# Seven-product (Strassen) GEMMs in three of four MLP layers, in four passes over the tokens

## The chip, the cores and the metric

The kernel runs on one core of one Trainium2 chip. The metric is the device time of one execution in microseconds (us). A run of the program is timed on its own; a profile of one execution shows the span from its first to its last instruction, and everything below that names a row is of that profile. The engines are TensorE (PE, whose weight loads the profile lists as PEld), VectorE (DVE), ScalarE (ACT), GpSimd (POOL) and SyncE (SP); here SP issues every DMA.

## The reference

The input is q, k and v, each 8 batches x 8 heads x 576 tokens x 64, in float32, and four weight matrices that arrive as float64 words. With 8 heads of 64 side by side a token has 512 features, and there are 4608 tokens.

```python
q_s = softmax(q, over the 64)          # per token and head
k_s = softmax(k, over the 576 tokens)  # per head and feature
x   = q_s @ (k_s.T @ v)                # per batch and head, then 4608 x 512
g   = h * sigmoid(1.702 * h),  h = x @ moe_w_in      # 512 -> 2048
x1  = g @ moe_w_out                                  # 2048 -> 512
g   = where(h >= 1, h, where(h <= -1, 0, (h + 1)**2 / 4)),  h = x1 @ moe2_w_in
out = g @ moe2_w_out
```

So four GEMMs of 4608 x 512 x 2048 carry the arithmetic. They are called in1, out1, in2 and out2 here.

## The kernel before, in words

The kernel is written in a tile framework. Python code lists the operations; the framework then fixes, ahead of time, an order of instructions for each engine (which need not be the order of the code), and puts in the semaphore waits. On the chip each engine works through its own list in that order.

Every GEMM operand is split into a high and a low part (`split`, L70 to L72: ACT rounds the high part into the type fp32r, DVE subtracts it from the source). A product is three matmuls: high x high, high x low, low x high. Each has a 128x128 weight and a moving operand of 512 columns.

The tokens are in nine blocks of 512. A step of the main loop belongs to a block and to one of 16 chunks of the hidden layer. `gemm1(s)` (L358 to L360) makes 12 matmuls into one PSUM tile `hps`, `act(s)` and `act_lo(s)` turn it into the split activation `gh`, `gl`, and `gemm2`, two steps behind, makes 12 matmuls (L400) that add the chunk's share to four accumulators. So the hidden activations never leave the core, and the 288 steps (nine blocks of the first MLP, then nine of the second) make 288 x 24 = 6912 matmuls. Only the block's output between the MLPs, `x1`, goes through DRAM.

Beside the steps runs a list of jobs (`at`, sorted by step): the attention of the next block (`chain`: loads, `k_max`, `k_col`, `k_sub`, `k_exp`, `k_v`, `q1` to `q4`), over the 16 steps before the block begins, and the weights. A weight chunk comes as 64-bit words (`load_w`), is made into float32 by one ACT and three DVE instructions (`conv_w`), and is split. The first MLP's weights are converted during the first two blocks, the second's during blocks 2 to 7, and those are kept in DRAM as float32 until the first MLP's last block.

Of the kernel before, what the change touches and what calls it, by code (L numbers as in the profile page):

```python
# [8 lines left out]
FP32 = mybir.dt.float32  # L9
# [9 lines left out]
def kernel(  # L19
# [25 lines left out]
    ACT_Q = (3,)  # L45
    ACT_KV = (0, 1)
    LOWEST = -3.4028234663852886e38
    FAST_K = (0, 1)
    RAW_W = 14
# [4 lines left out]
    wpool = ctx.enter_context(tc.tile_pool(name="w", bufs=2 * NM))  # L54
    xpool = ctx.enter_context(tc.tile_pool(name="x", bufs=2))
    kpool = ctx.enter_context(tc.tile_pool(name="k", bufs=3))
    qpool = ctx.enter_context(tc.tile_pool(name="q", bufs=4))
    qtpool = ctx.enter_context(tc.tile_pool(name="qt", bufs=1))
    sm1 = ctx.enter_context(tc.tile_pool(name="sm1", bufs=1))
    sm = ctx.enter_context(tc.tile_pool(name="sm", bufs=2))  # L60
    sgp = ctx.enter_context(tc.tile_pool(name="sg", bufs=2))
    gp = ctx.enter_context(tc.tile_pool(name="g", bufs=3))
    rawp = ctx.enter_context(tc.tile_pool(name="raw", bufs=1))
    stg = ctx.enter_context(tc.tile_pool(name="stg", bufs=4))
    dram = ctx.enter_context(tc.tile_pool(name="dram", bufs=1, space=bass.MemoryType.DRAM))
    ps_acc = ctx.enter_context(tc.tile_pool(name="ps_acc", bufs=1, space=bass.MemoryType.PSUM))
    ps_h = ctx.enter_context(tc.tile_pool(name="ps_h", bufs=2, space=bass.MemoryType.PSUM))
    ps_a = ctx.enter_context(tc.tile_pool(name="ps_a", bufs=2, space=bass.MemoryType.PSUM))

    def split(hi, lo, src):  # L70
# [3 lines left out]
    ident = const.tile([P, P], FP32, name="ident")  # L74
    NV = 2
    v_t = [const.tile([P, KR + 1, P + 1], FP32, name=f"v{i}") for i in range(NV)]
    kv_t = [const.tile([P, HP, P], FP32, name=f"kv{i}") for i in range(2)]

# [1 line left out]
    w_src = [(w1_in, w1_out), (w2_in, w2_out)]  # L80
    w_raw = {}
    st = {}
    w_f = {}
    w_sb = {}
    w2_dram = [
        [dram.tile([P, DM], FP32, name=f"w2_{io}_{m}") for m in range(NM)] for io in range(2)
    ]

    def load_w(ph, io, m):
        # as long as few weights are there, the others' room takes what comes in  # L90
        if ph == 0 and m < RAW_W:
            t = wpool.tile([P, DM], I64, tag="w", name="wraw")
        else:
            t = rawp.tile([P, DM], I64, tag="raw", name="wraw")
        if io == 0:
            nc.sync.dma_start(
                out=t.rearrange("p (k f) -> p k f", k=KD),
                in_=w_src[ph][0][:, m * P:(m + 1) * P].rearrange("(k p) f -> p k f", p=P),
            )
        else:  # L100
            nc.sync.dma_start(out=t, in_=w_src[ph][1][m * P:(m + 1) * P, :])
        w_raw[ph, io, m] = t

    def conv_w(ph, io, m):
        raw = w_raw.pop((ph, io, m))
# [3 lines left out]
        f = stg.tile([P, DM], FP32, tag="stg", name="wf")  # L109
        r = stg.tile([P, DM], U32, tag="stg", name="wr")  # L110
# [12 lines left out]
        w_f[ph, io, m] = f  # L123

    def store_w2(io, m):
        nc.sync.dma_start(out=w2_dram[io][m], in_=w_f.pop((1, io, m)))

    def load_w2(io, m):
        f = stg.tile([P, DM], FP32, tag="stg", name="wf")
        nc.sync.dma_start(out=f, in_=w2_dram[io][m])  # L130
        w_f[1, io, m] = f

    def split_w(ph, io, m):
        src = w_f[ph, io, m]
        t = wpool.tile([P, 2, DM], FP32R, tag="w", name="w")
        hi, lo = t[:, 0, :], t[:, 1, :]
        nc.scalar.activation(out=hi, in_=src, func=ACTF.Copy)  # L137
        w_sb[ph, io, m] = (hi, lo)

    def split_w_lo(ph, io, m):  # L140
        src = w_f.pop((ph, io, m))
        hi, lo = w_sb[ph, io, m]
        nc.vector.tensor_tensor(out=lo, in0=src, in1=hi.bitcast(FP32), op=ALU.subtract)  # L143

# [1 line left out]
    k_t, q_t = {}, {}  # L146

    # Of a batch's tokens, partition p has KR in a row; one more of the rest is in the first KT.
    def load_tokens(dst, src, together):
        if together:  # L150
            nc.sync.dma_start(out=dst[:, :, :KR], in_=src[:, :KR * P].rearrange("h (p r) d -> p h r d", r=KR))
        else:
            for i in range(2):
                nc.sync.dma_start(out=dst[:, i, :KR], in_=src[i, :KR * P].rearrange("(p r) d -> p r d", r=KR))
        nc.sync.dma_start(out=dst[:KT, :, KR], in_=src[:, KR * P:].rearrange("h p d -> p h d"))

    def load_k(b, hp):
        if b in FAST_K:
            t = wpool.tile([P, 2, KR + 1, D], FP32, tag="w", name="kr").rearrange("p h r d -> p r h d")
        else:  # L160
            t = kpool.tile([P, KR + 1, 2, D], FP32, tag="k", name="kt")
        nc.gpsimd.memset(t[KT:, KR], LOWEST)
        load_tokens(t.rearrange("p r h d -> p h r d"), k[b, 2 * hp:2 * hp + 2], b in FAST_K)
        k_t[b, hp] = t

    def load_v(b, hp):
        if b == 0 and hp >= NV:
            vt = wpool.tile([P, KR + 1, P + 1], FP32, tag="w", name="vf")
            nc.gpsimd.memset(vt[:, :, P:P + 1], 1.0)
        else:  # L170
            vt = v_t[hp % NV]
        load_tokens(
            vt[:, :, :P].rearrange("p r (h d) -> p h r d", h=2), v[b, 2 * hp:2 * hp + 2], False
        )
        st["v", b, hp] = vt

    def segs(t0, size):
        # a stretch of tokens, cut where a batch ends
        done = 0
        while done < size:  # L180
            b, s = divmod(t0 + done, S)
            n = min(size - done, S - s)
            yield done, n, b, s
            done += n

    def load_q(t):
        qt = qpool.tile([P, H, D], FP32, tag="q", name="qt")
        for off, n, b, s in segs(t * P, P):
            nc.sync.dma_start(
                out=qt[off:off + n], in_=q[b, :, s:s + n, :].rearrange("h p d -> p h d")  # L190
            )
        q_t[t] = qt

    def follow(ins, other):
        # keeps the exponentials together: ScalarE changes its table less often
        if other is not None:
            tc.add_manual_dep(
                getattr(ins, "ins", ins),
                getattr(other, "ins", other).name,
                mybir.DependencyInfo(mybir.DependencyClass.NoSync, mybir.DependencyReason.DATA),  # L200
                reason="exponentials together",
            )

    def k_max(b, hp):
        mx = sm1.tile([P, P], FP32, tag="mx", name="mx")
        nc.vector.tensor_reduce(  # L206
            out=mx.rearrange("p (h d) -> p h d", h=2),
            in_=k_t[b, hp].rearrange("p r h d -> p h d r"),
            axis=AX.X,
            op=ALU.max,  # L210
        )
        st["mx", hp] = mx

    def k_col(b, hp):
        pa = ps_a.tile([P, P], FP32, tag="a", name="pa")
        nc.tensor.transpose(out=pa, in_=st.pop(("mx", hp)), identity=ident)  # L216
        mc = sm.tile([P, 1], FP32, tag="mc", name="mc")
        nc.vector.tensor_reduce(out=mc, in_=pa, axis=AX.X, op=ALU.max)
        st["mc", hp] = mc
# [216 lines left out]
    for j in range(2, NB):  # L436
        run(0, j, 0, NM)
# [158 lines left out]
```

## Time and profile before

| what | value |
|---|---|
| three timed runs | 1718.35, 1720.17 and 1722.23 us, median 1720.17 |
| span of the profiled execution | 1716.3 us; the profile gives no time outside the span |
| runs' median less that span | 3.9 us |
| PE busy, matmuls | 98% of the span, 7576 matmul instructions |
| PE weight loads | 81% of the span |
| DVE, ACT busy | 52% and 40% |
| DMA | 109.08 MB on SP's queue, 22.2% of the 16 DMA engines' time |
| chain that ended last | PE 94%, DVE 3%, DMA 2%, ACT 1% |

A busy PE is not a PE at its peak: the end of a matmul is modelled, and the records of one after the other overlap. The pace of matmuls is read from the distance between two starts. The same holds for DVE, where the record of an instruction can reach into the next one's.

### The profile page before, as it was taken

How to read it: one execution, taken by the hardware profiler on the slowest of the kernel's cores; microseconds unless marked ns; L12 is line 12 of the kernel's file. 1: busy time of each engine (PE TensorE's matmuls, PEld its weight loads, DVE VectorE, ACT ScalarE, POOL GpSimd, SP SyncE). 2: the span in 40 equal slices, each digit the busy share in tenths (PEclk: the TensorE clock that was granted, in tenths of full speed). 3: DMA queues.
4: the chain of work that ended last, by engine and by line, in shares of the span. 5: the costliest groups of instructions: out<-in, count | busy, mean ns of one | idle time of the engine just before them, and what ended most of it. 6: DMA issues, size and time to landing. Idle time of an engine off the chain costs nothing.

```text
span 1716.3 us, 19507 instructions
## 1 busy us (share of the span) xinstructions
PE 1686.9 (98%) x7576; PEld 1383.0 (81%) x7576; DVE 895.9 (52%) x1511; ACT 679.2 (40%) x1033; POOL 8.0 (0%) x45
## 2 busy tenths in 40 slices
PE   5899999999999999999999999999999999999999
PEld 4688888888878888888788888888888888888887
DVE  7999438566565756542445343434343434343333
ACT  5885426445354554532444232323232323232222
POOL 0000000000000000000000000000000000000000
PEclk9999999999999999999999999999999999999999
DMA  8661315243241514210233010101010101000000
GB/s 221 174 197 56 85 55 147 59 137 79 68 128 45 151 40 125 56 62 19 92 99 99 1 49 1 50 1 50 0 50 0 50 0 48 2 13 13 3 23 25
DMA packets 155548, 110.32 MB, mean 64 GB/s; under 512 B 109888, under 2 KB 128320, under 8 KB 155456
## 3 DMA queue, kind: packets, MB, share of 16 engines
q1 hardware_dynamic: 155456, 109.08, 22.2%
q8 instruction: 59, 0.97, 0.2%
q14 instruction: 33, 0.27, 0.0%
HBM read 80.74 MB, written 28.31 MB: 64 GB/s over the span
## 4 chain that ended last, share of the span: by engine, by line
PE 94%; DVE 3%; DMA 2%; ACT 1%; issue 0%; SPq 0%; DVEq 0%; ACTq 0%
PE acc L400 44%; PE hps L358 15%; PE hps L360 15%; PE hps L359 15%; PE pk L247 3%; PE px L319 2%; DMA wraw<-in_moe_w_out_dram 1%; PE pt L303 1%; DMA wraw<-in_moe_w_in_dram 1%; DVE mx L206 0%; DVE wr L116 0%; PE pa L216 0%; DVE wr L115 0%; DMA x<-osb 0%; DVE w L143 0%
## 5 line engine op out<-in xcount | busy, mean ns | idle before, releaser
L358 PE MATMUL hps<-xh,w 128*128 128x512 f32 x1152 | 460.6, 400 | 0.0
L360 PE MATMUL hps<-xh,w 128*128 128x512 f32 x1152 | 450.5, 391 | 1.6 <-DVE w L143 1.4
L359 PE MATMUL hps<-xl,w 128*128 128x512 f32 x1152 | 449.8, 390 | 0.2 <-DVE xl L72 0.2
L400 PE MATMUL acc<-gh,w 128*128 128x512 f32 x1152 | 380.5, 391 | 3.2 <-ACT w L137 2.4
L400 PE MATMUL acc<-w,gh 128*128 128x512 f32 x1152 | 354.6, 389 | 0.0
L375 ACT ACTIVATE gh<-sg 128x512 fp32r<-128x512 f32 x288 | 181.6, 631 | 285.5 <-DVE sg L374 189.9
L373 DVE SCALAR_TENSOR_TENSOR sg<-sg 128x512 f32<-128x512 f32 x144 | 99.7, 692 | 360.6 <-ACT sg L372 360.6
L381 DVE TENSOR_TENSOR gl<-sg,gh 128x512 fp32r<-128x512 f32 x288 | 198.8, 690 | 133.6 <-ACT gh L375 131.9
L400 PEld LDWEIGHTS acc<-gh,w 128*128 128x128 f32 x1152 | 217.0, 188 | 49.3 <-ACT w L137 3.0
L360 PEld LDWEIGHTS hps<-xh,w 128*128 128x128 f32 x1152 | 216.2, 188 | 49.4 <-DVE w L143 3.2
L358 PEld LDWEIGHTS hps<-xh,w 128*128 128x128 f32 x1152 | 217.2, 189 | 47.8 <-issue 0.6
L359 PEld LDWEIGHTS hps<-xl,w 128*128 128x128 f32 x1152 | 216.5, 188 | 44.7 <-issue 1.1
L400 PEld LDWEIGHTS acc<-w,gh 128*128 128x128 f32 x1152 | 216.1, 188 | 44.9
L372 ACT ACTIVATE sg<-hps,half 128x512 f32<-128x512 f32 x144 | 99.1, 688 | 369.5 <-PE hps L360 369.5
L400 PE MATMUL acc<-gl,w 128*128 128x512 f32 x576 | 225.1, 391 | 0.0
L400 PE MATMUL acc<-w,gl 128*128 128x512 f32 x576 | 224.1, 389 | 0.0
L370 DVE TENSOR_TENSOR sg<-hps,sg 128x512 f32<-128x512 f32 x144 | 99.1, 689 | 211.6 <-ACT sg L369 211.2
L369 ACT ACTIVATE sg<-hps 128x512 f32<-128x512 f32 x144 | 85.9, 597 | 183.3 <-PE hps L360 182.7
L400 PEld LDWEIGHTS acc<-gl,w 128*128 128x128 f32 x576 | 108.6, 188 | 22.7 <-DVE gl L381 0.4
L400 PEld LDWEIGHTS acc<-w,gl 128*128 128x128 f32 x576 | 108.1, 188 | 22.5
L374 DVE TENSOR_TENSOR sg<-hps,sg 128x512 f32<-128x512 f32 x144 | 99.4, 690 | 4.4
L369 ACT ACT_TABLE_LOAD x43 | 55.2, 1283 | 53.5 <-PE hps L360 53.1
(61 smaller groups left out, 954.8 us busy)
## 6 DMA issues: line engine op xcount, KB each, us to landing
wraw<-in_moe_w_in_dram SPq DMA_DIRECT2D x32, 512.0 KB, 4.3
wraw<-in_moe_w_out_dram SPq DMA_DIRECT2D x32, 512.0 KB, 4.7
x<-osb SPq DMA_DIRECT2D x40, 256.0 KB, 2.7
xr<-x SPq DMA_DIRECT2D x36, 256.0 KB, 3.3
out_dram<-osb SPq DMA_DIRECT2D x36, 256.0 KB, 2.1
qt<-in_q_dram SPq DMA_DIRECT2D x32, 256.0 KB, 3.5
w<-wf SPq DMA_DIRECT2D x32, 256.0 KB, 4.1
wf<-w SPq DMA_DIRECT2D x32, 256.0 KB, 2.7
```

Of the source, the lines that this page charges most:

```text
L247: nc.tensor.matmul(out=pk, lhsT=kt[:n, r].rearrange("p h d -> p (h d)"), rhs=vt[:n, r, :], start=(r == 0), stop=(r == KR),)
L358: nc.tensor.matmul(out=hps, lhsT=wh[:, kk * P:(kk + 1) * P], rhs=xh[:, kk, :], start=(kk == 0), stop=False)
L359: nc.tensor.matmul(out=hps, lhsT=wh[:, kk * P:(kk + 1) * P], rhs=xl[:, kk, :], start=False, stop=False)
L360: nc.tensor.matmul(out=hps, lhsT=wl[:, kk * P:(kk + 1) * P], rhs=xh[:, kk, :], start=False, stop=(kk == KD - 1))
L369: nc.scalar.activation(out=sg, in_=hps, func=ACTF.Sigmoid, scale=1.702)
L370: nc.vector.tensor_tensor(out=sg, in0=hps, in1=sg, op=ALU.mult)
L372: nc.scalar.activation(out=sg, in_=hps, func=ACTF.Relu, scale=0.5, bias=half)
L373: nc.vector.scalar_tensor_tensor(out=sg, in0=sg, scalar=1.0, in1=sg, op0=ALU.min, op1=ALU.mult)
L374: nc.vector.tensor_tensor(out=sg, in0=hps, in1=sg, op=ALU.max)
L375: nc.scalar.activation(out=gh, in_=sg, func=ACTF.Copy)
L381: nc.vector.tensor_tensor(out=gl, in0=sg, in1=gh.bitcast(FP32), op=ALU.subtract)
L400: nc.tensor.matmul(out=acc[c], lhsT=a, rhs=b, start=(first and i == 0), stop=(last and i == 2))
```

## The change

The loop that makes in1 and out1, or in2 and out2, together is taken apart into four passes, each over all tokens, and three of the four GEMMs are cut into halves in each dimension and made by seven products in place of eight.

- **Pass in1** keeps nine blocks of 512 tokens, 16 steps each of 12 matmuls, the attention jobs (16 steps ahead, as before) and the conversion of the first weights. The activation is made for two chunks at once (1024 columns per instruction) and is stored in DRAM (`g0_dram`) with no split. As further jobs, one group every ten steps from step 17 on, the three other weight matrices are converted, added and subtracted into seven combinations each (`prep`), split, and stored in DRAM (`wp_dram`, seven tiles of [128, 2, 4, 512] float32 per matrix).
- **Passes out1, in2, out2** work on five blocks of tokens, in two halves of 464 or 460 tokens. Each loads its seven combined weights (`load_weights`) into the seven tiles of `wpool`, which pass in1 uses for its weights and as scratch. A product p has 48 matmuls of 460 or 464 columns; the operand's halves are combined on DVE (`operand`, `last_sum`), split, and the products are put together from PSUM on DVE and ACT (`post`). `pass_out` reads the hidden activations from DRAM, four loads to each of four quarters, into a pool of 16 tiles; `pass_in` stores them. out2's result stands transposed, so that PE transposes it (`turn`) before the store.
- `k_max` is three maxima of DVE in place of one reduction; all k tiles are loaded in long rows; `kv` is scaled on ACT; q's sums are all on DVE.

The core of the diff (of the removed lines, which are most of the kernel, only a few are shown):

```diff
+    HALVES = (464, 460, 460, 460, 460)
...
+    wpool = ctx.enter_context(tc.tile_pool(name="w", bufs=7))
...
+        def hl(w, si, p, src, neg=False):
...
+            t = s_hl[:, o:o + 1024].bitcast(FP32R).rearrange("p (a c f) -> p a c f", a=2, c=2)
+            hi, lo = t[:, 0], t[:, 1]
...
+                split(hi, lo, src)
+            nc.sync.dma_start(out=wp_dram[w, p][:, :, si, :], in_=t.bitcast(FP32).rearrange("p a c f -> p a (c f)"))
...
+            nc.vector.tensor_tensor(out=m2, in0=kr[:, 0:2], in1=kr[:, 2:4], op=ALU.max)
+            m1 = mx.rearrange("p (h d) -> p h d", h=2)
+            nc.vector.tensor_tensor(out=m1, in0=m2[:, 0], in1=m2[:, 1], op=ALU.max)
+            nc.vector.tensor_tensor(out=m1, in0=m1, in1=kr[:, KR], op=ALU.max)
...
+        def act(s):
+            j, m = divmod(s, NM)
+            hps = h_ps[0]
+            sg = sgp.tile([P, 2, TB], FP32, tag="sg", name="sg")
             nc.scalar.activation(out=sg, in_=hps, func=ACTF.Sigmoid, scale=1.702)
             nc.vector.tensor_tensor(out=sg, in0=hps, in1=sg, op=ALU.mult)
...
+            nc.sync.dma_start(out=g0_dram[j][m // 2], in_=sg)
...
+        for m in range(1, NM):
+            at(m - 4, load_w, m)
+            at(m - 2 + 0.1, conv_w, m)
+        for j in range(1, NB):
+            chain(j, j * NM - 16)
+        for i in range(12):
+            w, si = MATS[i // 4], i % 4
+            s0 = NM + 1 + i * 10
+            for h in range(2):
+                at(s0 - 3 + h, load_set, w, si, h)
+                at(s0 + 2 * h + 0.5, conv_set, h)
+            for part in range(4):
+                at(s0 + 4 + part + 0.5, prep, w, si, part)
...
+    def load_weights(w):
+        sl = {}
+        for p in PROD:
+            sl[p] = wslot()
+            nc.sync.dma_start(out=sl[p].bitcast(FP32), in_=wp_dram[w, p])
+        return sl
...
+            gpool = pool("g", 16)
+            rpool = pool("r", 8)
...
+                w = sl[p]
+                for m in range(2):
+                    for c in range(2):
+                        o = slice(c * 256 + m * P, c * 256 + (m + 1) * P)
+                        wh, wl = w[:, 0, i, o], w[:, 1, i, o]
+                        trio = ((wh, hi), (wh, lo), (wl, hi))
+                        for x, (a, b) in enumerate(trio):
+                            nc.tensor.matmul(
+                                out=z[:, m, :n], lhsT=a, rhs=b[:, c, :],
...
+            for s, (j, p, i) in enumerate(steps):
+                gemm(s)
+                if i == 2 and ph:
+                    turn()
+                if i == 3:
+                    post(j, p)
+                    if j + 1 < NJ:
+                        for qd in {2: ("11",), 7: ("12",), 3: ("22", "21")}.get(p, ()):
+                            load_g(j + 1, qd)
+                ready(s + LA)
...
+                def finish(h, a, b):
+
+                    t = new("ga")
+                    nc.scalar.activation(out=t, in_=h, func=ACTF.Relu, scale=0.5, bias=half)
+                    nc.scalar.activation(out=t, in_=t, func=ACTF.Square)
+                    nc.vector.scalar_tensor_tensor(
+                        out=t, in0=h, scalar=1.0, in1=t, op0=ALU.max, op1=ALU.min
+                    )
+                    nc.sync.dma_start(out=g1_dram[j, a, b, g], in_=t)
...
+            for j, g, p in seq:
+                if g == 0 and p == 3 and j + 1 < NJ:
+                    load_x(j + 1)
+                gemm(j, g, p)
+                post(j, g, p)
+                if g == 3 and j + 1 < NJ:
+                    ready(j + 1, p)
...
+    pass_out(0, "out1")
+    pass_in()
+    pass_out(1, "out2")
```

In `pass_out` a step (j, p, i) has 12 matmuls and i runs over four slices of the hidden layer; `ready` makes the operand of the step four ahead. In `pass_in` a step (j, g, p) has 12 matmuls and g runs over four groups of outputs; the order of its products is 1, 5, 6, 2, 3, 7, 4.

## Rows read from the trace of the kernel before

**Rows 1.** Page, its first line and busy time of the engines.

```profile
span 1716.3 us, 19507 instructions
PE 1686.9 (98%) x7576; PEld 1383.0 (81%) x7576; DVE 895.9 (52%) x1511; ACT 679.2 (40%) x1033; POOL 8.0 (0%) x45
```

The windows of group 2 are the startup, the first 16 steps, block 2 (with the attention of block 3 beside it), block 7 (with the attention of block 8, which has no batch of its own), and a block of the second MLP.

**Rows 2.** Windows: length, busy PE, PEld, DVE, ACT, POOL; PE clock, DMA share, GB/s.

```profile
0.00:35.68 35.68, 19.49 (x83) 14.37 (x83) 26.06 (x56) 16.50 (x42) 3.22 (x21) 0.95 0.82 213
35.68:141.13 105.45, 98.76 (x439) 77.75 (x439) 102.95 (x199) 83.61 (x129) 0.60 (x3) 0.98 0.60 172
...
240.90:340.73 99.83, 99.83 (x465) 82.02 (x464) 67.97 (x129) 52.16 (x71) 0.80 (x4) 1.00 0.40 103
...
743.86:836.42 92.56, 92.56 (x409) 75.08 (x408) 30.36 (x47) 28.11 (x47) 0.00 (x0) 1.00 0.13 40
...
923.46:1010.50 87.04, 87.04 (x385) 72.07 (x384) 38.25 (x58) 26.21 (x43) 0.00 (x0) 1.00 0.07 25
```

**Rows 3.** Timeline of PE in a block of the second MLP: start, length, engine, instruction.

```profile
1451.14 0.39 PE L358 MATMUL hps<-xh,w 128*128 128x512 f32 x1
1451.37 0.39 PE L359 MATMUL hps<-xl,w 128*128 128x512 f32 x1
1451.59 0.39 PE L360 MATMUL hps<-xh,w 128*128 128x512 f32 x1
```

**Rows 4.** Lines by form, PE: count, busy us in total, mean ns, idle before.

```profile
L358 PEld LDWEIGHTS hps<-xh,w 128*128 128x128 f32 x1152 | 217.2, 189 | 47.8 <-issue 0.6 <-DVE gl L381 0.2 <-ACT xh L71 0.2
...
L247 PEld LDWEIGHTS pk<-v,kt 128*128 128x128 f32 x240 | 32.6, 199 | 6.3 <-ACT kt L236 4.6
...
L303 PE MATMUL pt<-ident,qt 128*128 128x128 f32 x144 | 22.2, 278 | 4.0 <-DVE qt L291 4.0
```

**Rows 5.** Lines by form, DVE and ACT.

```profile
L381 DVE TENSOR_TENSOR gl<-sg,gh 128x512 fp32r<-128x512 f32 x288 | 198.8, 690 | 133.6 <-ACT gh L375 131.9
L375 ACT ACTIVATE gh<-sg 128x512 fp32r<-128x512 f32 x288 | 181.6, 631 | 285.5 <-DVE sg L374 189.9 <-DVE sg L370 94.4
...
L369 ACT ACTIVATE sg<-hps 128x512 f32<-128x512 f32 x144 | 85.9, 597 | 183.3 <-PE hps L360 182.7
...
L227 DVE TENSOR_TENSOR kt<-kt,pb 128x640 f32<-128x640 f32 x24 | 19.6, 816 | 1.0 <-PE pb L223 1.0
```

**Rows 6.** Lines by form, ACT alone, in block 2 (240.90 to 340.73 us).

```profile
L369 ACT ACT_TABLE_LOAD x7 | 9.0, 1283 | 10.1 <-PE hps L360 10.0
L282 ACT ACT_TABLE_LOAD x6 | 7.7, 1283 | 0.1
```

**Rows 7.** Timeline of DVE in a stretch in which it hardly stops.

```profile
73.38 0.68 DVE L370 TENSOR_TENSOR sg<-hps,sg 128x512 f32<-128x512 f32 x1
73.98 0.68 DVE L120 SCALAR_TENSOR_TENSOR wf<-wf,wr 128x512 uint32<-128x512 uint32 x1
```

**Rows 8.** DMA queue of SP, 34 to 50 us: packets, MB, share of 16 engines.

```profile
DMA packets 6597, 4.20 MB, mean 263 GB/s; under 512 B 4292, under 2 KB 6340, under 8 KB 6595
...
q1 hardware_dynamic: 6595, 4.18, 97.4%
```

**Rows 9.** The same, 836.42 to 923.46 us (rows of 2 KB).

```profile
q1 hardware_dynamic: 5472, 9.96, 39.0%
```

**Rows 10.** The same, 923.46 to 1619.78 us (rows of 2 KB).

```profile
q1 hardware_dynamic: 8640, 15.73, 6.5%
```

**Rows 11.** Timeline of SP, startup: start, length, DMA issued.

```profile
5.77 2.86 SPq L154 DMA_DIRECT2D v<-in_v_dram  x2
8.68 0.69 SPq L151 DMA_DIRECT2D kr<-in_k_dram  x1
```

**Rows 12.** Timeline of SP behind the first block's stores.

```profile
92.05 0.45 SPq L101 DMA_DIRECT2D wraw<-in_moe_w_out_dram  x1
109.33 2.77 SPq L412 DMA_DIRECT2D x<-osb  x4
112.15 0.43 SPq L96 DMA_DIRECT2D wraw<-in_moe_w_in_dram  x1
```

More of the change, by code (lines that the diff above doesn't have):

```diff
@@ L75 @@
[L75 to L102, printed above, removed]
@@ new lines @@
+    half = const.tile([P, 1], FP32, name="half")
+    PROD = (1, 5, 6, 2, 7, 3, 4)
+    MATS = ("out1", "in2", "out2")
+    wp_dram = {
+        (w, p): dram.tile([P, 2, 4, 512], FP32, name=f"wp_{w}_{p}") for w in MATS for p in PROD
+    }
+    g0_dram = [[dram.tile([P, 2, TB], FP32, name=f"g0_{j}_{m}") for m in range(NM // 2)] for j in range(NB)]
+    x1_dram = {
+        (j, a, b): dram.tile([P, 2, HALVES[j]], FP32, name=f"x1_{j}{a}{b}")
+        for j in range(NJ) for a in range(2) for b in range(2)
+    }
@@ L106, in conv_w, with wslot, flat, conv @@
+    g1_dram = {
+        (j, a, b, i): dram.tile([P, 2, HALVES[j]], FP32, name=f"g1_{j}{a}{b}{i}")
+        for j in range(NJ) for a in range(2) for b in range(2) for i in range(4)
+    }
+    def wslot():
+        return wpool.tile([P, 2, 4, 512], FP32R, tag="w", name="w")
+    def flat(t):
+        return t.rearrange("p a b c -> p (a b c)")
+    def conv(raw, f, r):
+        n = f.shape[-1]
         words = raw.bitcast(U32).rearrange("p (f two) -> p f two", two=2)
@@ L122, in conv_w @@
         )
[L123 to L175, printed above, removed]
@@ new lines, in q3 @@
+        def q3(t):
+            qt = q_t.pop(t)
+            j, c = divmod(t, NTB)
+            if c == 0:
+                st["qT", j] = qtpool.tile([P, HP, TB], FP32, tag="qT", name="qT")
+            pt = ps_a.tile([P, HP, P], FP32, tag="a", name="pt")
+            for hp in range(HP):
+                nc.tensor.transpose(
+                    out=pt[:, hp, :],
+                    in_=qt[:, 2 * hp:2 * hp + 2, :].rearrange("p h d -> p (h d)"),
+                    identity=ident,
+                )
+            nc.scalar.activation(out=st["qT", j][:, :, c * P:(c + 1) * P], in_=pt, func=ACTF.Copy)
@@ new lines, in q4 @@
+        def q4(j, hp):
+            px = ps_a.tile([P, TB], FP32, tag="a", name="px")
+            for off, n, b, s in segs(j * TB, TB, S):
+                nc.tensor.matmul(
+                    out=px[:, off:off + n],
+                    lhsT=kv_t[b % 2][:, hp, :],
+                    rhs=st["qT", j][:, hp, off:off + n],
+                    start=True,
+                    stop=True,
+                )
+            xh, xl = x_sb[j]
+            split(xh[:, hp, :], xl[:, hp, :], px)
+        x_sb = {}
@@ new lines, with at, chain, put @@
+        todo = []
+        def at(s, f, *a):
+            todo.append((s, len(todo), f, a))
+        def chain(j, c0):
+            b = j if j < B else None
+            def put(o, f, *a):
+                at(c0 + o, f, *a)
+            for i in range(4):
+                if b is not None:
+                    put(2 * i - 3, load_k, b, i)
+                    put(2 * i + 1, load_v, b, i)
+                    put(2 * i, k_max, b, i)
+                    put(2 * i + 1, k_col, b, i)
+                    put(2 * i + 2, k_sub, b, i)
+                    put(4.2 if i < 2 else 8.2, k_exp, b, i)
+                    put(2 * i + 5, k_v, b, i)
+                t = j * NTB + i
+                put(2 * i - 1, load_q, t)
+                put(2 * i + 2.2, q1, t)
+                put(4.3 if i < 2 else 8.3, q1e, t)
+                put(2 * i + 5.2, q2, t)
+                put(Q3[i], q3, t)
+                put(Q4[i], q4, j, i)
+            put(11, alloc_x, j)
@@ new lines @@
+        for i in range(HP):
+            load_q(i)
+            load_v(0, i)
+        for f, a in jobs.get(-1, ()):
+            if f is not conv_w:
+                f(*a)
+        for hp in range(HP):
+            k_max(0, hp)
+            k_col(0, hp)
+            k_sub(0, hp)
+            k_exp(0, hp)
+        for i in range(HP):
+            q1(i)
+            q1e(i)
+            k_v(0, i)
+            q2(i)
+            q3(i)
+            if i == 0:
+                conv_w(0)
+        for hp in range(HP):
+            q4(0, hp)
@@ new lines, with split, tt @@
+        for f, a in jobs.get(-1, ()):
+            if f is conv_w:
+                f(*a)
+        for s in range(NB * NM):
+            gemm1(s)
+            if s % 2 == 1:
+                act(s)
+            for f, a in jobs.get(s, ()):
+                f(*a)
+    def split(hi, lo, src):
+        nc.scalar.activation(out=hi, in_=src, func=ACTF.Copy)
+        nc.vector.tensor_tensor(out=lo, in0=src, in1=hi.bitcast(FP32), op=ALU.subtract)
+    def tt(o, x, y, op):
+        nc.vector.tensor_tensor(out=o, in0=x, in1=y, op=op)
```

789 lines of the change are left out of this document (429 added, 360 removed).

## The prediction, made before the change was run

> **What bounds the kernel now.** I read the page first. PE is busy for 98% of the span, and DVE, ACT and DMA are far below [rows 1]. The windows by block then show what a stage costs. A block of the second MLP has nothing but 384 matmuls and takes 87.04 us [rows 2]: 226.7 ns each, which is also the distance between two starts in the timeline [rows 3]. The clock there is granted in full, and at 2.4 GHz 512 columns stream in 213.3 ns. So a matmul costs its columns and 13.3 ns. Block 2 of the first MLP has the same 384 and the attention of a later block, and takes 99.83 us: attention costs PE 12.8 us a block. Block 7, with queries alone, takes 92.56 us: 5.5. The startup is 35.7 us. Matmuls of 512 columns make 6912 x 0.2267 = 1567 us of 1716, so only fewer columns can gain much, and the question is what else becomes late when the rest stays.
>
> **Columns saved.** In a pass a block of tokens has 7 x 48 = 336 matmuls. With 464 columns one costs 193.3 + 13.3 = 206.7 ns, with 460, 191.7 + 13.3 = 205.0. A pass is 336 x 0.2067 + 4 x 336 x 0.2050 = 345 us. A GEMM was 1728 x 0.2267 = 391.7. Three save 140 us.
>
> The trace has no fp32r matmul under 512 columns, so the 205.0 has two bounds. The weight load before each is recorded with 189 ns [rows 4]; if it were what sets the pace, with 38 ns of something behind it, 226.7 would stay. Against that, 240 loads of the same shape in `k_v` fill only 32.6 us of busy time, 136 ns each, though each is recorded with 199 [rows 4]: the records overlap, so their length is not their price. I take 205.0. The other bound is in the rivals.
>
> The Trainium skill, TensorE: Matmul & The Clock Gate, section Back-to-back issue gap, gives a single matmul 2.5 ns above its columns, and says that in a stream both the weight load and the matmul set the spacing. The row for 512 columns has 13.3 ns, so the 2.5 is not borne out; by it the three passes would take 5040 x 10.8 ns = 54 us less, an estimate from that page. The second half is the mechanism of the weight-load rival.
>
> **Pass in1.** It has half of a block's matmuls (192 x 0.2267 = 43.5 us), but all of the attention and a fresh load of weight work. Per block, for each unit:
>
> PE: 43.5 + 12.8 = 56.3 us.
>
> DVE: 690 ns for 512 elements and 816 for 640 [rows 5] are 0.98 ns an element, but where work is queued an instruction of 512 starts every 0.60 us [rows 7]; so by estimate 1024 cost 1.10, 920 1.00, 640 0.73, 256 0.35 and 128 0.22. Attention is 4 x 1.9 for k (the three maxima 0.8) and 4 x 2.6 for q, and 2.4 for the splits: 20. The activation is 8 x 1.10 = 9. A group of weight work is six conversions of 1024 and eleven sums and splits of 512, 13.2 us, and 1.6 groups fall on a block: 21. Together 50 us. Block 0 has 60 conversions and splits of 512 instead, 36 us: 65 together.
>
> ACT: 13 table loads as now [rows 6] are 16.7; the rest is scaled from 597 ns (out of PSUM) and 631 ns for 512 elements [rows 5]: sigmoids of 1024 8 x 1.0, exponentials 5.4, copies out of PSUM 7.3, weights 10.4. Together 48 us.
>
> DMA: k, v and q 3.4 MB, the stored activation 4.2, the 11.2 stores of split weights 0.52 each, 5.9, and 3.4 of raw words: 16.8 MB. What the 16 DMA engines carry while busy is 4.18 MB / (16 x 0.974 us) = 268 GB/s where most packets are small [rows 8], 9.96 / (87.04 x 0.39) = 293 with rows of 2 KB at two fifths load [rows 9] and 15.73 / (696 x 0.065) = 348 with the same rows at low load [rows 10]. So 63, 57 or 48 us.
>
> Four units between 48 and 60 us, each in a fixed order and each fed by the others, don't overlap fully. The floor is PE's 56.3. The upper bound is DMA's 63 with the attention chain behind it in the open, another 12.8: 75. I take 63, since v and q come in short pieces. What is late then is `k_v` and `q4`, hence the next block's x; PE has no second GEMM to fill the wait as `gemm2` did. Sum: block 0 65 (DVE), blocks 1 to 6 63 each, block 7 55, block 8 (no attention) 45: 543 us. With the floor it is 56.3 x 7 + 49 + 43.5 = 487, with the upper bound 622.
>
> The Trainium skill, DMA: Bandwidth & Descriptors, section Bandwidth, measured 341 GB/s with 1 MB and 425 with 16 MB in one transfer. No row here reaches the latter; by 341 DMA would need 49 us a block (an estimate), and PE would be the bound, as in the clean rival.
>
> **The passes beside PE.** In `pass_out` a block of tokens has 28 splits, 16 sums of operands and 5 of results on DVE, 49 x 1.0 us (920 elements) = 49 of 69 us. In `pass_in` it has 47; ACT 43 x 0.95 = 41. PE stays the bound, and operands are made four steps ahead. In `pass_in` the last group of a block carries 20 DVE instructions against 17.2 us of matmuls, with a lead of one group; I give it 7 us in all. The trace has no Square. If it needed a table of its own, 160 loads of 1.28 us would put ACT at 205 + 205 us, 60 above the pass; Relu and Copy, which alternate now, need none, so I take nothing. Traffic is 7.5 MB in and 1.9 MB out a block: 32 us of 69 at 293 GB/s. out2 has 160 transposes at 22.2 / 144 = 0.154 us [rows 4], at most 25; part overlaps, 20.
>
> **The three boundaries.** A pass needs seven weights of 2.1 MB (7.2 us at 293 GB/s) and quarters of the operand of 1.9 MB (6.5 us). From in1 to out1, three weight tiles come free during the last 12 steps and three with the scratch before that: 8 us of wait. From out1 to in2 the tiles come free one product (9.8 us) at a time: 6. From in2 to out2 all seven are in use until the last group, 17 us before the end, and each product of 9.8 us then asks for a weight and a quarter, 13.7 us: 3.9 x 4 less the lead, 10. These rest on SP issuing the loads before the old pass's last stores have gone, though the code has them behind. The framework does reorder: SP issues v loads ahead of a k load that the code has before them [rows 11]. Behind a DMA that waits stands all of SP's queue.
>
> **Sum.** 35.7 + 543 + 8 + 345 + 6 + 352 + 10 + 345 + 20 + 8 (the last sum, transposes, copy and store) = 1672.7 us of span, against 1716.3. The runs' median lies 3.9 us above the span, so 1677 against 1720.17.
>
> **The rivals.**
>
> *Clean*: DMA keeps up, in1 runs at PE's floor, the boundaries hide. 35.7 + 487 + 3 x 345 + 20 + 8 + 5 + 3.9 = 1595. For it: DVE ran 95% busy and more in the first 16 steps (102.95 of 105.45 us) and PE still 94% [rows 2]. Against it: that stretch had 172 GB/s, this one asks for 300 at PE's floor.
>
> *Pass in1 starves*: 75 us a block, 1677 + 79 = 1756, slower. It decides from 69 us a block on. For it, the 300 GB/s against 268 to 293 measured.
>
> *The weight load sets the pace*: 226.7 ns at 460 columns too. 5040 x 21.7 ns = 109 us, so 1786. It decides where a matmul of 460 columns takes over 213 ns. For it the recorded 189 ns, close under the pace; against it the overlap in `k_v`.
>
> *Weights behind the stores*: SP holds the weight loads behind the old pass's last stores, and each pass waits for 14.7 MB and a quarter, 57 us. Three less the 24 counted: 1677 + 147 = 1824. It decides from 22 us a boundary on. For it: SP stood from 92 to 109 us at stores whose data was late, and the next weight load went out 0.05 us behind them [rows 12]. Against it [rows 11], and that a wait lasts only as long as the fixed order and the chip disagree.
>
> **How the numbers follow.** Forecast 0.52 (its own range 1630 to 1715: in1 500 to 575, boundaries 10 to 40), clean 0.15, in1 starved 0.14, weight load 0.09, stores 0.10. To leave out no more than 2 in 10 the range goes from the clean case to the starved one, 1590 to 1760. A change under 0.2% is about what a measurement of this kernel can't tell from none. Faster gets the first two and the gentler end of starvation, 0.71; same 0.03; slower 0.26.
>
> **What would show it.** The distance between starts of 460-column matmuls (205 or 227 ns); the length of 16 steps in pass in1 (56, 63 or 75 us) with DMA's share near 0.9; PE's idle time at the three boundaries and what SP waits for there; a table load at Square. The prediction is wrong if a pass takes over 365 us inside, or in1 over 585.

## The result: slower by 0.6%, and the profile after

The changed kernel takes 1730.41 us (1727.85 to 1731.54, 4 runs), the kernel before 1719.26 us (1717.89 to 1722.23, 4 runs). The ratio is 1.0063, with an interval of 1.0049 to 1.0077: slower, by little and clearly. The forecast was 1677 and faster.

The page of the changed kernel, first line, engines and slices:

```profile
span 1726.1 us, 20570 instructions
...
PE 1603.0 (93%) x7584; PEld 1381.3 (80%) x7584; DVE 1234.0 (71%) x1541; ACT 874.1 (51%) x1037; POOL 9.3 (1%) x45
...
PE   5899999998999399999999899999993899999997
...
PEclk9999999999999699999999899999997899999999
DMA  8778888888788952725547433424239563442601
...
q1 hardware_dynamic: 240336, 329.30, 58.4%
```

PE is busy for 84 us less than before [rows 1], and the span is 10 us longer: 94 us more of PE's time are idle. Two digits in PE's line show most of it, the two 3s: there the granted clock falls too, and DMA's digit is 9. The windows put numbers on these places (columns as in [rows 2]): startup, block 0 and block 3 of the first pass, its last block, the stretch between the first and the second pass, a block of the second and of the third, the stretch between the third and the fourth, and a block of the fourth.

```profile
0.00:37.80 37.80, 17.53 (x73) 12.23 (x73) 26.59 (x69) 16.70 (x31) 3.25 (x21) 0.95 0.87 210
37.80:104.92 67.12, 60.66 (x275) 46.55 (x274) 63.52 (x126) 51.04 (x72) 0.80 (x4) 0.97 0.76 225
218.41:275.34 56.93, 56.86 (x273) 46.27 (x272) 45.73 (x84) 38.13 (x52) 0.80 (x4) 1.00 0.78 247
515.24:560.21 44.97, 44.97 (x194) 36.02 (x192) 22.73 (x26) 15.05 (x19) 0.00 (x0) 1.00 0.86 317
560.21:590.46 30.25, 0.40 (x3) 0.00 (x1) 1.25 (x2) 2.00 (x2) 0.00 (x0) 0.59 1.01 420
664.56:734.66 70.10, 70.10 (x337) 63.13 (x337) 52.54 (x50) 28.92 (x30) 0.00 (x0) 1.00 0.45 135
1028.90:1099.00 70.10, 70.10 (x337) 63.02 (x336) 50.01 (x48) 41.41 (x44) 0.00 (x0) 1.00 0.38 135
1310.73:1345.00 34.27, 0.37 (x3) 0.00 (x1) 3.01 (x4) 3.01 (x3) 0.00 (x0) 0.54 0.99 390
1421.70:1495.30 73.60, 73.60 (x370) 66.56 (x369) 52.62 (x50) 33.26 (x39) 0.00 (x0) 1.00 0.45 129
```

In the blocks of the second, third and fourth pass shown here PE does not stop. Between the passes it stands for 30.25 and 34.27 us while the DMA engines are full. (Such a stretch is counted from the start of the last matmul to the start of the next one, so it holds one matmul of 0.2 us.) The chain of waits of the changed kernel says what they carry first (start, length, what), from the end of the first pass on:

```profile
560.64 1.03 ACT sg L391
561.70 1.24 DVE sg L392
562.95 0.32 SPq L393
563.32 0.42 SPq L501
563.84 0.64 SPq L501
564.53 0.49 SPq L501
565.11 0.44 SPq L501
565.60 23.75 DMA gq<-g
589.43 0.98 ACT hi L488
590.44 1.14 DVE lo L489
591.62 8.39 PE z L592 x28
```

The last activation of the old pass is stored at L393. Then SP issues four weight loads at L501, and only then the first operand tile of the new pass, which lands 23.75 us later. The timeline of SP at the other place shows the same order: last store (L742), four weights, operands.

```profile
1315.88 0.51 SPq L742 DMA_DIRECT2D g<-ga  x1
1316.48 2.46 SPq L501 DMA_DIRECT2D w<-wp_out  x4
1319.04 5.13 SPq L551 DMA_DIRECT2D gq<-g  x4
```

The transfers of that first stretch, 560.4 to 590.4 us, in the view of the DMA queues:

```profile
DMA packets 1709, 12.62 MB, mean 421 GB/s; under 512 B 151, under 2 KB 877, under 8 KB 1069
q1 hardware_dynamic: 1709, 12.62, 101.2%
w<-wp_out SPq DMA_DIRECT2D x4, 2048.0 KB
```

Four weights are 8.4 MB, 20 us at 421 GB/s. That is the size of the wait, if the operand has to queue behind them.

The terms of the sum beside what the trace shows, in us:

| term | predicted | measured | difference |
|---|---|---|---|
| startup | 35.7 | 37.8 | +2.1 |
| first pass | 543 | 522.4 | -20.6 |
| first to second pass | 8 | 30.25 | +22.2 |
| second pass | 345 | 354.4 | +9.4 |
| second to third pass | 6 | 2.6 and 6.2 inside the first block | +2.8 |
| third pass without that | 352 | 357.0 | +5.0 |
| third to fourth pass | 10 | 34.27 | +24.3 |
| fourth pass | 365 | 371.1 | +6.1 |
| tail | 8 | 10.0 | +2.0 |
| span | 1672.7 | 1726.1 | +53.4 |

The stretches between the passes took 49 us more than predicted, the three passes some 20 more, and the first pass 20 less; the rest is small.

### The profile page after: what moved, and what is told of

It reads as the page before. It is cut to its first block, busy times and chain, and to the rows that moved or that the text cites. A ratio compares the mean times of both kernels' runs of the same rounds, so it can differ in the third digit from the quotient of the medians.

```text
span 1726.1 us, 20570 instructions
## 1 busy us (share of the span) xinstructions
PE 1603.0 (93%) x7584; PEld 1381.3 (80%) x7584; DVE 1234.0 (71%) x1541; ACT 874.1 (51%) x1037; POOL 9.3 (1%) x45
## 4 chain that ended last, share of the span: by engine, by line
PE 67%; DMA 4%; DVE 2%; ACT 1%; issue 1%; SPq 0%; ACTq 0%; DVEq 0%
PE z L592 40%; PE z L720 20%; DMA gq<-g 3%; PE hps L383 2%; PE hps L385 1%; PE hps L384 1%; DMA xq<-x 1%; PE pt L615 1%; PE px L354 1%; DVE sg L392 0%; SPq L501 0%; ACT ga L737 0%; PE pk L305 0%; ACT ga L738 0%; DVE w L125 0%
## 5 line engine op out<-in xcount | busy, mean ns | idle before, releaser
L592 PE MATMUL z<-hi,w 128*128 128x460 f32 (+1 forms) x2240 | 658.2, 374 | 63.8 <-ACT hi L488 63.8
L592 PEld LDWEIGHTS z<-hi,w 128*128 128x128 f32 x2240 | 422.9, 189 | 112.3 <-ACT hi L488 64.6
L488 ACT ACTIVATE hi<-gq 128x920 fp32r<-128x920 f32 (+1 forms) x280 | 273.0, 975 | 452.5 <-PE z L592 367.0
L489 DVE TENSOR_TENSOR lo<-gq,hi 128x920 fp32r<-128x920 f32 (+1 forms) x280 | 312.1, 1115 | 214.5 <-ACT hi L488 213.4
L592 PE MATMUL z<-lo,w 128*128 128x460 f32 (+1 forms) x1120 | 417.3, 373 | 0.8 <-DVE lo L489 0.8
L720 PE MATMUL z<-hi,w 128*128 128x460 f32 (+1 forms) x1120 | 327.6, 373 | 3.5 <-ACT hi L488 2.3
L383 PE MATMUL hps<-xh,w 128*128 128x512 f32 x576 | 237.1, 412 | 7.3 <-ACT w L124 3.5
L720 PEld LDWEIGHTS z<-hi,w 128*128 128x128 f32 x1120 | 211.7, 189 | 29.0 <-ACT hi L488 2.6
L592 PEld LDWEIGHTS z<-lo,w 128*128 128x128 f32 x1120 | 212.3, 190 | 25.2 <-DVE lo L489 1.7
L385 PE MATMUL hps<-xh,w 128*128 128x512 f32 x576 | 230.5, 400 | 1.1 <-DVE w L125 1.1
L384 PE MATMUL hps<-xl,w 128*128 128x512 f32 x576 | 229.4, 398 | 0.0
L720 PE MATMUL z<-lo,w 128*128 128x460 f32 (+1 forms) x560 | 209.3, 374 | 6.5 <-DVE lo L489 6.5
L492 DVE TENSOR_TENSOR gq<-gq 128x920 f32<-128x920 f32 (+1 forms) x160 | 175.9, 1113 | 2.1
L383 PEld LDWEIGHTS hps<-xh,w 128*128 128x128 f32 x576 | 109.1, 190 | 35.7 <-ACT w L124 5.5
L385 PEld LDWEIGHTS hps<-xh,w 128*128 128x128 f32 x576 | 109.0, 189 | 27.6 <-DVE w L125 2.2
L384 PEld LDWEIGHTS hps<-xl,w 128*128 128x128 f32 x576 | 109.1, 189 | 24.3 <-issue 0.6
L720 PEld LDWEIGHTS z<-lo,w 128*128 128x128 f32 x560 | 106.3, 190 | 19.2 <-DVE lo L489 7.2
```

Of the source, the lines that this page charges most:

```text
L383: nc.tensor.matmul(out=hps, lhsT=wh, rhs=xh[:, kk, :], start=(kk == 0), stop=False)
L384: nc.tensor.matmul(out=hps, lhsT=wh, rhs=xl[:, kk, :], start=False, stop=False)
L385: nc.tensor.matmul(out=hps, lhsT=wl, rhs=xh[:, kk, :], start=False, stop=(kk == KD - 1))
L492: nc.vector.tensor_tensor(out=o, in0=x, in1=y, op=op)
L592: nc.tensor.matmul(out=z[:, m, :n], lhsT=a, rhs=b[:, c, :], start=(p in OPENS and i == 0 and c == 0 and x == 0), stop=(i == 3 and c == 1 a ...
L720: nc.tensor.matmul(out=z[:, m, :n], lhsT=a, rhs=b[:, c, :], start=(p in OPENS and c == 0 and x == 0), stop=(c == 1 and x == 2), skip_group ...
```

## The experiments

**What stands between the passes.** Operands first: the order of the loads alone is changed.

```
-    sl = load_weights(wname)            # seven weights, then the quarters
+    sl = {}
...
-    for qd in ("11", "12", "22", "21"):
-        load_g(0, qd)
+    for qd, ps in (("11", (1,)), ("12", (5,)), ("22", (6,)), ("21", (2, 7, 3, 4))):
+        load_g(0, qd)
+        for p in ps:
+            load_weight(sl, wname, p)
...
     # pass_in: load_x(0) ahead of its seven weights
```

> In the changed kernel TensorE stands still for 30.3 us between the first and the second pass (560.2 to 590.5) and for 34.3 us between the third and the fourth (1310.7 to 1345.0). This kernel only changes the order in which SP issues loads: at the first block of an out pass each operand quarter goes ahead of the weights of the products that need it later (quarter 11, then weights 1; 12, 5; 22, 6; 21, then 2, 7, 3, 4), and in the third pass the operands are asked for ahead of the weights. Theory A, the first operand quarter stands in the DMA queues behind four weight loads of 2.1 MB (8.4 MB at the 421 GB/s that the stretch 560.4 to 590.4 shows is 20 us): the standstill becomes 10 us between the first two passes and 12 us before the fourth, out passes otherwise as they are, so the time falls by 42 us, to about 1688. Theory B, the passes end late whatever comes first, because all 12.2 MB of operands and weights (29 us at 421 GB/s) must land before a pass can run at its pace: the wait moves into the first block of each pass, each out pass as a whole ends when it did, and the time stays at 1720 or above. Theory C, the wait is for space (slots that come free only with the last product of the old pass) and not for the queue: the standstills stay above 25 us, 1725.

Measured: 1685.87 us, ratio to the kernel before 0.9804 (0.9788 to 0.982). One edit of order turns 0.6% slower into 2% faster. The standstill between the first two passes is 4.5 us, with 2.5 more a matmul later, where 10 were expected. The weights' bytes are hidden behind the second pass, which takes 355.9 us instead of 354.4: theory B falls, and theory C too, as both standstills are under 25 us. The 6.2 us inside the third pass are gone. Before the fourth pass 19.6 us are left where 12 were expected. The timeline of SP in this run shows why:

```profile
1284.98 0.56 SPq L499 DMA_DIRECT2D w<-wp_out  x1
1288.65 0.51 SPq L747 DMA_DIRECT2D g<-ga  x1
1289.25 0.60 SPq L499 DMA_DIRECT2D w<-wp_out  x1
1289.95 19.37 SPq L554 DMA_DIRECT2D gq<-g  x15
```

The framework had put the weights of products 6 and 2, whose tiles come free early, ahead of the operands again (the program has them behind). The windows of the two standstills in this run show DMA full only in the second:

```profile
562.65:567.13 4.48, 0.39 (x2) 0.00 (x1) 1.22 (x1) 2.00 (x2) 0.00 (x0) 1.00 0.70 275
1283.51:1303.09 19.58, 0.37 (x3) 0.00 (x1) 3.00 (x4) 3.01 (x3) 0.00 (x0) 0.63 0.98 358
```

**The weights taken away.** The same question from the other side: the changed kernel, in which the second pass's weights stay for the third and fourth. It leaves out the loads of those passes' own weights: all three multiply by the second pass's.

```
+    kept = {}
+
     def load_weights(w):
-        sl = {}
+        if kept:
+            return kept
+        sl = kept
```

> The seven weight tiles of the second pass are loaded once and serve the third and the fourth pass too, so that the loads of 14.7 MB at each of the two later boundaries are left out (third and fourth pass so multiply by the second pass's weights). Theory A, the operands stand behind weight loads: the standstill of 30 us before the second pass stays, that of 34.3 us before the fourth shrinks to the chain of the last block's tail, store and load, about 9 us, and the 6.2 us wait in the third pass's first block goes; 31 us less, about 1699. Theory B, the standstill before the fourth pass is the store of the last activations and its way back through DRAM: it stays above 25 us, and the time above 1715.

Measured: 1700.7 us in one run. Before the second pass PE stands for 32.0 us (30.25 in the changed kernel), before the fourth for 11.7; the third pass's first block has no wait over 2.4 us. Theory A, to 2 us. With no weight in the queue the operand's tile lands in 4.85 us instead of 24.85, as the chains of waits say, first this run's, then the changed kernel's:

```profile
1312.03 4.85 DMA gq<-g
```

```profile
1319.04 24.85 DMA gq<-g
```

**The rest of the order.** The weights of products 6, 2, 7, 3 and 4 are held behind the operands by an ordering edge, without a semaphore.

```
+    def behind(load, other):
+        tc.add_manual_dep(
+            getattr(load, "ins", load), getattr(other, "ins", other).name,
+            mybir.DependencyInfo(mybir.DependencyClass.NoSync, mybir.DependencyReason.DATA),
...
-            load_weight(sl, wname, p)
+            o = load_weight(sl, wname, p)
+            if p not in (1, 5):
+                behind(o, d)             # d: the last load of that quarter
```

> With operands first, 19.6 us of standstill were left before the fourth pass (1283.5 to 1303.1): there the weights of products 6 and 2 still stood in SP ahead of the operand quarters, since their slots came free earlier. Here the weights of products 6, 2, 7, 3 and 4 are held, in SP's order alone, behind the operand quarters that stand ahead of them in the program. Theory A, weights in the queue are what is left: two loads less in front, 4.2 MB at 421 GB/s = 10 us, a standstill of 9.6 us, and 1676. Theory B, what is left is the last block's activations, their stores and the space they free: a standstill of 17 to 20 us, and 1684 to 1688. Theory C, the weights of product 6 now come too late, and what the standstill loses shows as a wait inside the first block: 1686 or more.

Measured: 1677.98 us, 0.9763 (0.9747 to 0.978). The standstill before the fourth pass is 11.2 us, 8.4 less, and the time 7.9 less than with operands first. Theory A. No wait appears inside the fourth pass's first block. The windows of the first stretch (with the matmul in it and the wait behind that) and of the second:

```profile
561.98:568.95 6.97, 1.15 (x3) 0.29 (x2) 2.35 (x2) 2.00 (x2) 0.00 (x0) 0.67 0.79 270
1283.10:1294.29 11.19, 0.36 (x3) 0.00 (x1) 3.00 (x4) 3.01 (x3) 0.00 (x0) 0.72 0.67 205
```

What is left is seen in the chain of waits of this run: the last block's activations, their store, one load, and the split.

```profile
1284.99 1.07 ACT ga L752
1286.08 0.98 ACT ga L753
1287.09 1.13 DVE ga L754
1288.23 0.51 SPq L757
...
1288.84 4.34 DMA gq<-g
...
1293.26 0.98 ACT hi L488
1294.27 1.14 DVE lo L489
```

Whether the load could go ahead of the last store wasn't tried: the new pass's tiles lie where the old pass's were.

**The price of a matmul.** Left is the second term, 208.7 ns between starts at 460 columns against 205.0. Three rows of the changed kernel's PE timeline show it, 0.2 us from one start to the next; over 1343 pairs of the second pass the mean is 208.68, and nine in ten of the single steps lie between 203 and 214.

```profile
699.64 0.37 PE L592 MATMUL z<-hi,w 128*128 128x460 f32 x1
699.85 0.38 PE L592 MATMUL z<-lo,w 128*128 128x460 f32 x1
700.07 0.57 PE L592 MATMUL z<-hi,w 128*128 128x460 f32 x2
```

The first guess was the layout of the weight tiles.

```
-    wpool.tile([P, 2, 4, 512], FP32R, ...)
+    wpool.tile([P, 4, 2, 512], FP32R, ...)
```

> The weight tiles are laid out as in the kernel before: the two parts of a 512-wide row of weights beside each other (4 x 2 x 512) instead of 8 KB apart (2 x 4 x 512); nothing else changes. Theory A, the place of the weights in the tile costs the 3.7 ns a matmul by which 460 columns (208.7) and the 512 columns of the first pass (232.4 against 226.7 in the kernel before) are over the price in the prediction: the pitches go back to 205.0 and 226.7, which is 3.7 ns x 5040 = 19 us in the three passes and 5.7 ns x some 2300 = 13 us in the first, so about 1700. Theory B, the layout is nothing to TensorE: pitches stay within 0.5 ns of 208.7 and 232, and the time within 4 us of the changed kernel's 1730.

Measured: 1732.27 us in one run, 208.7 ns at 460 columns in the second pass as before, and 233.3 in the first pass. Theory B: this layout does nothing to the pace.

The second was the width. `HALVES = (384,) * 6`, in the changed kernel's order:

> Blocks of six times 384 columns in place of 464 and four times 460; the same work. In the changed kernel a matmul of 460 columns takes 208.7 ns from one to the next in the three passes. If a matmul costs its columns at 2.4 GHz and a fixed 17 ns, the pitch is 177 ns and a block of 336 matmuls takes 59.5 us. If the pass is held by something that does not shrink with the columns (a weight load of 189 ns beside it, or the issue of a pair), the pitch stays above 189 ns and a block above 63.5 us; six blocks are then over 381 us a pass against 354.5, and the time is over 1800. With 17 ns fixed the three passes are some 6 us each longer for their matmuls (6 x 59.5 against 5 x 70.1), and the time is 1750 at most.

Measured: 1724.66 us in one run; 384 columns take 173.5 ns, that is 160.0 and 13.5, close to the 13.3 that 512 columns cost over theirs [rows 3]. 173.5 lies under the 189 ns of a weight load's record [rows 4], so that record sets no pace.

Then with the better order, the same six halves, and two runs with other widths (`HALVES` alone is changed):

> The order of the run before with blocks of six times 384 columns. 384 columns took 173.5 ns from one matmul to the next in the run of six halves (160.0 for the columns and 13.5), 460 columns 208.7 to 209.1 (191.7 and 17): a pass of six blocks of 336 has 349.8 us of matmuls, one of five 352.1 to 353. Theory A, the two edits add: 2 to 3 us in each of three passes, 7 us less than with the order alone, about 1669. Theory B, what six blocks add in other work (VectorE, ScalarE, more and smaller stores) takes it back: the same as with the order alone within 2 us.

Measured: 1671.25 us (1668.65 to 1672.49), 0.9718 (0.9704 to 0.9733), 6.7 us under the run with operands ahead of the weights on the same chip. The edits add, and no run below is faster by more than runs of one kernel differ. Three rows of its PE timeline:

```profile
699.76 0.33 PE L603 MATMUL z<-hi,w 128*128 128x384 f32 x1
699.93 0.33 PE L603 MATMUL z<-lo,w 128*128 128x384 f32 x1
700.10 0.51 PE L603 MATMUL z<-hi,w 128*128 128x384 f32 x2
```

> The order of the run before and blocks of 416, 400, 384, 384, 368 and 352 columns, to read the price of a matmul at each width. Theory A, the price is columns at 2.4 GHz and 13.5 ns for every width up to some point between 384 and 460: 186.8 at 416, 180.2 at 400, 173.5 at 384, 166.8 at 368, 160.2 at 352. Theory B, widths that are a multiple of 128 alone have 13.5 and the others 17: 190.3, 183.7, 173.5, 170.3, 163.7. Theory C, a floor near the 189 ns of a weight load's record: 352 and 368 cost no less than 173.

> The order of the run before and blocks of 448 and four times 464 columns. Theory A, up to some width 13.5 ns and above it more: 448 lies on one side, 200.2 or 203.7 or more, and 464 stays at 211 to 213 (17.7 to 19.5 over its columns). Theory B, a multiple of 64 alone is cheap: 200.2 at 448, 211 to 213 at 464.

Measured: 1684.44 and 1678.1 us in one run each. In the third pass 189.5 ns at 416 columns, 182.3 at 400, 175.6 at 384, 168.9 at 368, 160.4 at 352; 203.5 at 448 and 211.2 at 464. Theory C fell, and no rule of width held: 384 columns cost 2 ns more than in the run before, with single steps from 173 to 181. What differed for them was the tile: there its two rows lay 416 columns apart. So this was tried alone, in four runs, by the row length of the tiles `hi` and `lo` (in one of them in the second pass alone):

```
-    hi = rpool.tile([P, 2, NX], FP32R, ...)[:, :, :n]
+    hi = rpool.tile([P, 2, 416], FP32R, ...)[:, :, :n]     # or 512, or 480; lo too
```

> Six halves of 384 columns with the operands ahead of the weights, and one edit: the moving tiles hi and lo have rows of 416 columns (1664 bytes) in place of 384 (1536 bytes). Theory A, the distance of the rows makes the uneven steps: the pitch goes from 173.5 to 175.6, 2.1 ns x 6048 = 13 us more, about 1684. Theory B, the other tiles of the kernel with mixed sizes made it (the stores, the additions): the pitch stays at 173.5 and the time at 1671.

> Open is why 460 columns cost 17 ns over the columns and 384 columns 13.5, while 384 columns in tiles with a row of 416 columns cost 15.6 to 16.1 and step unevenly. Here, in the order with operands ahead of the weights, the moving tiles hi and lo of the second pass alone have rows of 512 columns (2048 bytes) in place of 464 (1856 bytes), five blocks of 464 and 460 columns as before; the fourth pass keeps rows of 464 and is the comparison inside the run. Theory A, the distance of the two rows of the moving tile makes the extra: 205.0 ns at 460 in the second pass, 209.1 in the fourth, 7 us less, about 1671. Theory B, the column count itself makes it: 209.1 in both passes, 1678. Theory C, the place of the whole tile (its start) makes it: 512-column rows in a ring of tiles land elsewhere and the pitch changes by another amount.

> Six halves of 384 columns, operands ahead of the weights, and rows of 512 columns (2048 bytes) in the moving tiles hi and lo. Rows of 384 columns (1536 bytes, no gap between the two rows) gave an even 173.5 ns, rows of 416 (1664 bytes, a gap of 128 bytes) an uneven 175.7. Theory A, a row distance that is a multiple of 512 bytes is what makes it even: 173.5, and about 1671. Theory B, any gap between the rows makes it uneven: 175.7, and about 1684.

> Halves of 464 and four times 460, operands ahead of the weights, rows of 480 columns (1920 bytes) in the moving tiles. Rows of 464 (1856 bytes) gave 208.7 to 209.6, uneven, rows of 512 (2048 bytes) an even 206.7. Theory A, only a multiple of 512 bytes is even: 208 to 210 and uneven in all three passes, 1678 within 3. Theory B, the longer the gap the better: between 206.7 and 208.7, about 1674.

Measured (mean distance of starts in the second and the third pass, steps over 300 ns left out; the column of steps has the middle nine tenths of them; the two times of 1671.25 and 1677.98 us are medians of four runs, the others are one run each):

| columns | row, bytes | ns | over columns / 2.4 GHz | steps, ns | time, us |
|---|---|---|---|---|---|
| 384 | 1536 | 173.6, 173.5 | 13.5 | 173, 174 | 1671.25 |
| 384 | 2048 | 173.5, 173.6 | 13.5 | 173, 174 | 1670.67 |
| 384 | 1664 | 175.7, 175.8 | 15.7 | 173 to 181 | 1683.89 |
| 460 | 1856 | 208.7, 208.8 | 17.1 | 203 to 214 | 1677.98 |
| 460 | 1920 | 208.9, 208.9 | 17.2 | 203 to 215 | 1673.38 |
| 460 | 2048 (second pass alone) | 206.7, 208.8 | 15.0 in the second | 206, 207 in the second | 1673.11 |

Adding 128 bytes to a row of 1536 costs 13 us, and adding 512 costs nothing: so it is not that any gap costs. In this table the even steps come at 1536 and 2048 bytes, both multiples of 512, and not at 1664, 1856 or 1920. For 460 columns rows of 2048 bytes take away 2.0 of the 3.7 ns; the other 1.7 stay open.

A row of a multiple of 512 bytes is not enough, though. In the run with rows of 2048 bytes in the second pass, the first block has 464 columns, in the same tiles: its steps go 215, 205, 215, 205, 210.0 in the mean and 16.7 over the columns, where 460 columns have 15.0. And 352 columns in rows of 1664 bytes took 160.4 to 161.1 ns, 13.7 to 14.4 over theirs, where 384 have 15.7. So the width has a part in it as well.

Nor is it shown that the distance itself is the cause. A matmul reads one of the two rows (`rhs=b[:, c, :]`), and with the row length the place at which a row starts changes too. With rows of 1664 bytes the extra is not spread: six matmuls, three on the first row and three on the second, start 174, 174, 175, 181, 176 and 173 ns apart, in step after step. With rows of 480 columns the six steps are 203, 209, 209, 208, 208 and 215 ns in the second pass, and 208, 208, 215, 203, 209 and 209 in the third: the same row length, and the first and second row have changed parts. That speaks for the place (theory C of the run with the second pass alone), and no run separates it from the distance.

The run with rows of 480 had the pitch at 460 columns that theory A expected and still took 1673 us in its one run. Its first pass began 2.2 us earlier than in the run with rows of 464 (37.9 against 40.1 us), its block of 464 columns ran at 209.8 ns instead of 212.9 in the third pass (1 us), and the runs of one kernel lie up to 4 us apart (1676.23 to 1680.09 with rows of 464).

## Why the prediction was wrong

**The step that failed is the three boundaries.** It took the loads of a new pass as pairs, one weight and one quarter for each product (13.7 us against the 9.8 of a product), and so found that only the differences had to be waited for: 8, 6 and 10 us. The code asks for all seven weights ahead of the first quarter. Ahead of the second and of the fourth pass, the four whose tiles come free late go out behind the old pass's last store, and the first quarter behind them: 30.25 and 34.27 us, and with 8.8 at the other boundary 73 where 24 were summed. With the order that the prediction had taken for granted these are 4.1 (and 2.8 a matmul later) and 11.2, near what it priced. Its other premise, loads issued before the last stores, does not hold even there: the operand goes out behind the last store (1288.23 and 1288.84 us). The time is then 1678, the forecast 1677; but that nearness is partly luck, since two other terms were off by 20 us in opposite ways.

**The rival nearest in mechanism** is the one of the weights behind the stores, at 0.10; by its time, 1824, it was far off. It decides from 22 us a boundary on, and the mean of the three was 24.4. Its sign was right, its mechanism half right: four weights did stand behind the last store, but a pass doesn't wait for its 14.7 MB and need not. With the same bytes in another order the waits shrink to 7 and 11.2 us. What hurts is the first operand behind the weights; that is why it is about 20 us more and not 57 each time.

**Columns saved** was right in kind: 460 columns took 208.7 to 209.6 ns and not 226.7, so the weight-load rival falls. The size was off, 209 for 205, some 19 us over the 5040 matmuls, because the extra of 512 columns was carried to a width and a row length where it doesn't hold. The Trainium skill, TensorE: Matmul & The Clock Gate, section Back-to-back issue gap, gives 2.5 ns above the columns for a single matmul. No fp32r stream here met it: the least extra was 13.3 ns.

**Pass in1** was taken at 63 us a block, DMA's bound at 268 GB/s. Blocks 1 to 4 take 56.7 to 57.7 us, at PE's floor of 56.3, and blocks 5 and 6 64.5 and 60.7: 353 us for the six against 378. In block 5 PE waits 1.9 us for the maxima of k and 2.9 us for q, both made by DVE. DMA carried 247 GB/s in block 3 for 56.93 us, 14.1 MB where 16.8 were reckoned, and was not full (0.78). The last block moved 317 GB/s, the standstills 390 to 420: rates measured at low load or with short packets [rows 8 to 10] are no ceiling. The Trainium skill, DMA: Bandwidth & Descriptors, section Bandwidth, has 425 GB/s for 16 MB in one transfer, and the prediction set it aside; the 421 GB/s here, with four loads of 2.1 MB in a row, lie close to it. The starved rival falls. The clean one is right on blocks 1 to 4 and wrong on the boundaries; for the whole first pass 522 us lie nearer to the forecast's 543 than to its 487. The upper bound of 622 does not follow from its own 75 us a block: six blocks with 12 more each give 615.

**The passes beside PE** hold: DVE is busy for 50 to 53 us of 70, ACT for 29 to 41, PE for all of it. No table load appears in the third pass; a Square of 920 elements takes 0.97 us. The transposes of the fourth pass cost 3.5 us a block (73.6 against 70.1), 17.5 where 20 were given.

## What to carry to other kernels

Where a kernel is split into passes that go through DRAM, price the boundary by what stands in front of the first operand in the queue, in order, and not by the sum of bytes: here four weights of 2.1 MB ahead of one quarter turned a gain of 2% into a loss. A framework may reorder loads by when their tiles come free, so read the order that it made from SP's timeline, and pin it if needed. And when a GEMM is cut to an odd width, time it with more than one row length of its operand's tiles in SBUF as well as at more than one width: no rule for either came out of these runs.

## What the runs showed of the hardware that was not expected

- The pace of fp32r matmuls changes with the row length of the moving tile: 173.5 ns at 1536 and 2048 bytes, 175.7 at 1664, for the same 384 columns. It is not the row length alone: in rows of 2048 bytes 460 columns took 206.7 ns, 15.0 over the columns, and 464 columns 210.0, 16.7 over.
- After a standstill the first matmuls are slow. The windows of the changed kernel behind the one of 30.25 us (columns as above) have a granted clock of 0.50, the lower level of 1.2 GHz, then 0.93, then 1.00; 464 columns start 0.39 us apart at first, 0.21 later. The chain of waits has 28 of them in 8.39 us, where 28 x 0.211 would be 5.9: this standstill cost some 2.5 us more than its length. Behind the one of 34.27 us the first 5 us have 0.50 as well, and behind the 11.2 us of the kernel with operands ahead of the weights the first 4.7 us have 0.58.

```profile
591.62:596.00 4.38, 4.38 (x11) 3.79 (x12) 4.05 (x4) 1.98 (x3) 0.00 (x0) 0.50 1.09 342
596.00:600.01 4.01, 4.01 (x19) 3.55 (x18) 3.77 (x5) 1.96 (x2) 0.00 (x0) 0.93 1.09 342
600.01:664.00 63.99, 63.99 (x306) 56.95 (x305) 48.35 (x46) 26.18 (x27) 0.00 (x0) 1.00 0.61 187
```

- In the first pass matmuls of 512 columns start 233.1 to 233.3 ns apart in every run, and 232.4 to 233.3 in the last block, which has no attention beside it, against 226.7 in the second MLP of the kernel before [rows 3], with rows of 2048 bytes in both. In the changed kernel's last block the steps alternate between 229 or 230 and 237 or 238; in that second MLP all are 226 or 227. Weight layout and load order don't change it. The cause is open.
